# Block-masked attention into a rational feed-forward layer: the weight clamp folded into an Abs, the last tile's maxima chained in PSUM, and twelve units moved behind the switch

## The chip, the cores and the metric

The kernel runs on one core of a Trainium2 chip. Its time is the device time of one execution in microseconds; a profiled execution also gives a span, from its first to its last instruction. The engines of the core run beside each other and wait for one another through semaphores: TensorE (PE) multiplies matrices into PSUM, VectorE (DVE) and ScalarE (ACT) read and write PSUM and SBUF, GpSimd (POOL) works on SBUF alone, and SyncE (SP) issues the DMAs. PSUM has eight banks of 512 float32 columns by 128 partitions.

## What is computed

Eight batches of eight heads, 576 positions, head size 64. Attention is masked by blocks of 64 positions, and its output, 4608 tokens of 512 features, goes through a feed-forward layer of width 2048 whose activation is a rational function.

```python
scores = scale * np.matmul(q, k.transpose(0, 1, 3, 2))
mask = block_i >= block_j
scores = np.where(mask, scores, -1000000000.0)
scores = scores - np.max(scores, axis=-1, keepdims=True)
attn = np.exp(scores)
attn = attn / (np.sum(attn, axis=-1, keepdims=True) + 1e-09)
x = np.matmul(attn, v)            # then heads side by side: 4608 x 512
h = x @ w_in
P = a[0] + a[1] * h + a[2] * h**2 + a[3] * h**3
Q = 1.0 + np.abs(b[0]) * np.abs(h) + np.abs(b[1]) * h**2
out = (P / (Q + 1e-6)) @ w_out
```

The two weight matrices arrive as float64; q, k and v are float32.

## The kernel before

Every matrix product of the layer is made of three: each operand is split into a high part and the rest, and high x high, high x rest and rest x high are added in PSUM.

**The planner.** The kernel is written as operations handed to a class `Plan`: each has an engine, an estimated cost, a priority (a small number goes early) and the buffers that it reads and writes. `order()` (line 94) plays the program through with these costs: on each engine it starts the operation of the lowest number that can start, gives it its buffers, and so fixes the order of instructions on every engine. A `Buf` may take a slot of a second pool, a quota, so that one use can't take all PSUM banks: QA (5) for attention, QH (1) and QO (2) for the first product and the output of the first stage, QH1 (2), QO1 (4) and QR1 (2) for the second stage. `gate(pri, ahead)` (line 349) makes an operation wait until the attention's scores of number `pri - ahead` have been issued; the attention runs through the numbers 0 to 319, ten for each of 32 pairs of heads.

**Attention.** For a pair of heads, `load` brings q, k and v, `prep` transposes q and k on PE and splits them, and `scores` (line 443) works through five tiles of queries. A tile's scores are in one PSUM bank, those of the last tile (t = 4, 576 keys) in two pieces of 288. DVE takes the negated maximum of each piece (L467); for the last tile a third instruction (L471) takes the smaller of the two. ACT makes the Exp with this bias and the row sums (L475), POOL scales the probabilities by the reciprocal (L489, L495), PE transposes them (L516), ACT and DVE split them (L531, L533), and `pv` (line 540) multiplies them with v and writes the result to scratch in HBM (`xscr`, L572). There is one buffer of probabilities for each of the five tiles. The transposes have the number of their tile less 6 (line 501).

**Weights.** `place` (line 576) turns a block of 128 x 512 float64 weights into the two float32 parts with integer operations on the two words: ACT's Abs of the upper word (L585), a maximum with the constant WMIN on POOL (L587), then shifts and masks on DVE (L589 to L599), one more ACT and one POOL operation. There are 32 blocks: 16 for the first half of the hidden features, which stay in SBUF (`wA`), and 16 for the second half, which go to scratch.

**The layer.** The hidden features are split in halves of 8 x 128. The first stage (`ffn0`, line 665) runs beside attention: 18 chunks of 256 tokens, four units each. A unit is two groups of 12 matmuls of 256 columns into one bank (L698), the activation (`wide`, line 633: ACT L635, L636, L646, L649, L658; POOL L638, L640, L659; DVE L642 to L655), and 12 matmuls of 512 columns into the chunk's two output banks (L717). The chunk's sums go to scratch (`pscr`, L725). Units have numbers from 50 to 325 and on: the last 14 of the 72 come after the attention's end. When attention is over, `switch` (line 757) gives its SBUF to the second half's weights (`wB`, loaded at L773), two x tiles (`xx`) and one tile for stored sums (`pp`). The second stage (`ffn1`, line 780) then takes nine chunks of 512 tokens in order, each with eight units of one 128-feature group (12 matmuls of 512 columns at L805, 12 at L821); it loads the two stored sums of a chunk into the one `pp` tile (L830), adds them (L834) and stores the result (L838).

Of the kernel before, what the change touches and what calls it, by code (L numbers as in the profile page):

```python
# [23 lines left out]
CT = 256  # L24
# [11 lines left out]
WMIN = struct.unpack("<f", struct.pack("<I", (1023 - 127) << 20))[0]  # L36
# [21 lines left out]
class Op:  # L58
    __slots__ = ("eng", "c", "d", "fn", "pri", "deps", "outs", "bufs", "n", "ready", "at", "end", "seq")


LATENCY = {"PE": 90.0, "ACT": 40.0, "DVE": 40.0, "POOL": 90.0, "SP": 60.0, "-": 0.0}


class Plan:
# [5 lines left out]
    def op(self, eng, cd, fn, rd=(), wr=(), pri=0.0, after=()):  # L71
        o = Op()
        o.eng, (o.c, o.d), o.fn, o.pri, o.seq = eng, cd, fn, pri, len(self.ops)
# [14 lines left out]
        if eng in ("ACT", "DVE") and any(b.quota for b in bufs):  # L88
            o.pri -= 4
# [4 lines left out]
    def order(self):  # L94
# [16 lines left out]
        def startable(o):  # L111
            t, need = o.ready, {}
            for b in o.bufs:
                if b.slot is None:
                    need.setdefault(b.pool, []).append(0)
# [9 lines left out]
        while left:  # L125
# [41 lines left out]
            o.at = t  # L167
            if e == "SP":
# [55 lines left out]
def attn_ffn_kernel(  # L224
# [24 lines left out]
    QA, QH, QO, QH1, QO1, QR1 = (Pool([None] * n) for n in (5, 1, 2, 2, 4, 2))  # L249
# [37 lines left out]
    NM = tiles(att, 6, [128, 2, 2], F32, "nm")  # L287
# [155 lines left out]
    def scores(p, s, t):  # L443
# [5 lines left out]
        for j in range(2):  # L449
# [4 lines left out]
            bks = []  # L454
            for i, (c0, w) in enumerate(pieces(t)):
                ww = max(w, 256)
                bank = Buf(banks, QA, 1)
                bks.append(bank)

                def sc(bank=bank, c0=c0, ww=ww, kq=kq):  # L460
# [3 lines left out]
                o_ = aop("PE", mm(2, ww), sc, rd=kk, wr=[bank], pri=pri, after=kqmask[p % 2, j] if p < 2 else ())  # L464
                if not i:
                    gates[p * 10 + t * 2 + j] = o_
                aop("DVE", dve(w), lambda bank=bank, i=i, j=j, w=w: nc.vector.reduce_max(  # L467
                    out=nm.t[:nq, j, i:i + 1], in_=bank.t[:nq, :w], axis=AX.X, negate=True),
                    rd=[bank], wr=[(nm, j, i)], pri=pri)
            if t == 4:  # L470
                aop("DVE", (141, 160), lambda j=j: nc.vector.tensor_tensor(  # L471
                    out=nm.t[:, j, 0:1], in0=nm.t[:, j, 0:1], in1=nm.t[:, j, 1:2], op=ALU.min),
                    rd=[(nm, j, 1)], wr=[(nm, j, 0)], pri=pri)
            for i, (c0, w) in enumerate(pieces(t)):
                aop("ACT", act(w, True, 1, True), lambda i=i, j=j, c0=c0, w=w, bank=bks[i]: nc.scalar.activation(  # L475
                    out=pt.t[:nq, j, c0:c0 + w], in_=bank.t[:nq, :w], func=AF.Exp,
                    bias=nm.t[:nq, j, 0:1], scale=1.0, accum_out=sm.t[:nq, j, i:i + 1]),
                    rd=[bks[i], (nm, j, 0)], wr=[(pt, j, i), (sm, j, i)], pri=pri, after=first)
# [399 lines left out]
```

## Time and profile before

| | us |
|---|---|
| time, median of 3 (1412.52 to 1414.75) | 1413.2 |
| the profiled execution | 1413.04 |
| its span | 1410.8 |
| PE busy | 1270.7 (90%) |
| DVE busy | 1012.6 (72%) |
| POOL busy | 963.6 (68%) |
| ACT busy | 906.4 (64%) |

The page of the profile shows the span in forty slices of about 35 us; each digit is the busy share of an engine in tenths. Other views give busy time by stretch, by line, the waits with the instruction that ended them, and the instructions in order of time. A matmul's duration in a row includes its way through the array, and the next one starts before it ends; the work of a group of matmuls is therefore read from the length of the whole group.

### The profile page before, as it was taken

To read this page: it belongs to the slowest core of one execution; us is meant where nothing else is said; L and a number is where in the kernel's file an instruction comes from. 1 tells how busy PE (TensorE), PEld (TensorE's weight loads), DVE (VectorE), ACT (ScalarE), POOL (GpSimd) and SP (SyncE) were. 2 spreads that over 40 slices of the span, in tenths; PEclk is the share of its full clock that TensorE was granted. 3 is DMA by queue.
4 is the path that set the end of the run, shared out by engine and by line. 5 is a ranking of instruction groups with operands and counts; after the bars stand their busy time and mean duration, and the time that the engine had idled before them with its cause. 6 is when DMAs were issued, how large, how long until landed. Compare 5 with 4: busy or idle time off the path is not lost.

```text
span 1410.8 us, 23662 instructions
## 1 busy us (share of the span) xinstructions
PE 1270.7 (90%) x7616; PEld 1113.0 (79%) x7616; DVE 1012.6 (72%) x2045; ACT 906.4 (64%) x2246; POOL 963.6 (68%) x1245
## 2 busy tenths in 40 slices
PE   4767789999999999999999999678999999999996
PEld 3657688888888888888888899567888888888875
DVE  4778887777878887787886776444576667666764
ACT  4767776776777777677777677334555556555553
POOL 4789987777778778678787677334566566555653
PEclk9878999999999999999999999888999999999998
DMA  8868576666567576666765652840032323222321
GB/s 195 224 183 222 137 193 176 163 189 190 161 185 195 154 201 185 176 166 170 192 187 154 166 149 72 299 170 31 16 117 63 99 80 120 91 89 87 93 60 45
DMA packets 230811, 206.17 MB, mean 146 GB/s; under 512 B 131872, under 2 KB 189216, under 8 KB 230688
## 3 DMA queue, kind: packets, MB, share of 16 engines
q1 hardware_dynamic: 230624, 204.66, 51.5%
q8 instruction: 61, 1.00, 0.3%
q14 instruction: 62, 0.51, 0.1%
q0 software_dynamic: 64, 0.00, 0.0%
HBM read 100.67 MB, written 46.14 MB: 104 GB/s over the span
## 4 chain that ended last, share of the span: by engine, by line
PE 42%; POOL 26%; DVE 11%; ACT 8%; issue 5%; DMA 5%; SPq 1%; POOLq 0%; DVEq 0%; ACTq 0%
POOL vpl L432 3%; POOL ua L640 2%; POOL p3a L495 2%; POOL ua L587 2%; POOL gla L659 2%; PE psb L821 2%; PE psf L805 2%; PE psg L805 2%; POOL ub L587 2%; POOL glb L659 1%; PE psc L821 1%; POOL vb L638 1%; POOL ub L640 1%; POOL p2a L495 1%; PE psa L717 1%
## 5 line engine op out<-in xcount | busy, mean ns | idle before, releaser
L659 POOL TENSOR_TENSOR glb<-sa,ghb 128x512 fp32r<-128x512 f32 x62 | 80.0, 1290 | 103.5 <-ACT ghb L658 103.0
L659 POOL TENSOR_TENSOR gla<-sb,gha 128x512 fp32r<-128x512 f32 x58 | 75.0, 1292 | 66.1 <-ACT gha L658 65.7
L432 POOL TENSOR_TENSOR vpl<-vra,vph 128x256 fp32r<-128x256 f32 (+1 forms) x128 | 78.2, 619 | 22.6 <-ACT vph L430 15.9
L640 POOL TENSOR_TENSOR ub<-va,ub 128x512 f32<-128x512 f32 x63 | 82.2, 1304 | 4.8
L638 POOL TENSOR_SCALAR va<-ub,bab 128x512 f32<-128x512 f32 x63 | 49.3, 783 | 47.7 <-ACT ub L635 45.9
L640 POOL TENSOR_TENSOR ua<-vb,ua 128x512 f32<-128x512 f32 x59 | 77.4, 1313 | 4.7
L646 ACT ACTIVATE va<-ub,qcb 128x512 f32<-128x512 f32 x63 | 45.7, 725 | 53.8 <-POOL ub L640 53.7
L658 ACT CAST ghb<-sa 128x512 fp32r<-128x512 f32 x62 | 38.4, 620 | 58.6 <-DVE sa L655 58.4
L638 POOL TENSOR_SCALAR vb<-ua,bab 128x512 f32<-128x512 f32 x59 | 48.2, 818 | 39.7 <-ACT ua L635 34.7
L646 ACT ACTIVATE vb<-ua,qcb 128x512 f32<-128x512 f32 x59 | 42.7, 724 | 35.7 <-POOL ua L640 35.7
L658 ACT CAST gha<-sb 128x512 fp32r<-128x512 f32 x58 | 35.8, 617 | 39.7 <-DVE sb L655 32.3
L587 POOL TENSOR_SCALAR ua<-ua 128x512 f32<-128x512 f32 x19 | 37.7, 1987 | 9.9 <-ACT ua L585 9.5
L430 ACT CAST vph<-vra 128x256 fp32r<-128x256 f32 (+1 forms) x128 | 39.4, 324 | 4.5 <-DMA vra<-in_v_dram 3.0
L651 DVE SCALAR_TENSOR_TENSOR ub<-ub,va 128x512 f32<-128x512 f32 x27 | 20.4, 756 | 16.5 <-ACT va L649 16.4
L651 DVE SCALAR_TENSOR_TENSOR ua<-ua,vb 128x512 f32<-128x512 f32 x23 | 18.6, 810 | 12.8 <-ACT vb L649 11.0
L587 POOL TENSOR_SCALAR ub<-ub 128x512 f32<-128x512 f32 x13 | 26.2, 2018 | 0.2
L649 ACT ACTIVATE va<-va 128x512 f32<-128x512 f32 x37 | 23.5, 634 | 0.5
L642 DVE TENSOR_TENSOR sb<-sb,psh 128x512 f32<-128x512 f32 x10 | 6.8, 685 | 21.9 <-ACT sb L636 21.9
L649 ACT ACTIVATE vb<-vb 128x512 f32<-128x512 f32 x35 | 22.2, 633 | 0.6
L653 DVE SCALAR_TENSOR_TENSOR va<-ub,va 128x512 f32<-128x512 f32 x27 | 21.8, 807 | 0.4
L589 DVE TENSOR_SCALAR ua<-ua 128x512 int32<-128x512 int32 x19 | 12.8, 673 | 12.4 <-POOL ua L587 12.3
L642 DVE TENSOR_TENSOR sb<-sb,psf 128x512 f32<-128x512 f32 x10 | 6.8, 684 | 20.0 <-ACT sb L636 20.0
(1597 smaller groups left out, 5882.1 us busy)
## 6 DMA issues: line engine op xcount, KB each, us to landing
xscr<-xsa SPq DMA_DIRECT2D x32, 320.0 KB, 2.9
qra<-in_q_dram SPq DMA_DIRECT2D x64, 144.0 KB, 3.0
qra<-in_k_dram SPq DMA_DIRECT2D x64, 144.0 KB, 2.9
ppa<-pscr SPq DMA_DIRECT2D x18, 512.0 KB, 4.2
vra<-in_v_dram SPq DMA_DIRECT2D x64, 128.0 KB, 2.4
xscr<-xsa SPq DMA_DIRECT2D x32, 256.0 KB, 2.7
kqaa<-hl0a SPq DMA_DIRECT2D x48, 144.0 KB, 3.1
kqab<-hl0a SPq DMA_DIRECT2D x48, 144.0 KB, 3.1
```

What stands on the lines that cost most here:

```text
L430: aop("ACT", (0.833 * n + 110, 0.833 * n + 200), lambda vh=vh, src=src: nc.scalar.copy(out=vh, in_=src()), rd=rd, wr=[("v", i, 0)], pri=pr ...
L432: aop("POOL", pool(n, True), lambda vh=vh, vl=vl, src=src: nc.gpsimd.tensor_tensor(out=vl, in0=src(), in1=vh.bitcast(F32), op=ALU.subtract ...
L495: aop("POOL", pool(n - 64), lambda jj=jj: nc.gpsimd.tensor_scalar(out=pt.t[:nq, jj, 64:n], in0=pt.t[:nq, jj, 64:n], scalar1=rc.t[:nq, jj:j ...
L587: op("POOL", pool(512), lambda: nc.gpsimd.tensor_scalar(out=at.t, in0=at.t, scalar1=WMIN, scalar2=1.0, op0=ALU.max, op1=ALU.mult), wr=[at] ...
L638: op("POOL", pool(512, False, 2), lambda: nc.gpsimd.tensor_scalar(out=vt.t, in0=ut.t, scalar1=b1, scalar2=b0, op0=ALU.mult, op1=ALU.add), ...
L640: op("POOL", pool(512, True), lambda: nc.gpsimd.tensor_tensor(out=ut.t, in0=vt.t, in1=ut.t, op=ALU.mult), rd=[vt], wr=[ut], pri=pri)
L646: op("ACT", act(512, False, 1), lambda: nc.scalar.activation(out=vt.t, in_=ut.t, func=AF.Ln, bias=qcb), rd=[ut, "qcb"], wr=[vt], pri=pri)
L649: op("ACT", act(512, False), lambda: nc.scalar.activation(out=r0.t, in_=vt.t, func=AF.Exp, scale=-1.0), rd=[vt] if rpsum else [], wr=[r0], ...
L658: op("ACT", act(512, False), lambda: nc.scalar.copy(out=gh.t, in_=st.t), rd=[st], wr=[gh], pri=pri)
L659: op("POOL", pool(512, True), lambda: nc.gpsimd.tensor_tensor(out=gl.t, in0=st.t, in1=gh.t.bitcast(F32), op=ALU.subtract), rd=[st, gh], wr ...
L805: nc.tensor.matmul(h.t, lhsT=w[:, dc, fs], rhs=x.t[:, dc, hl, :], start=(dc == 0 and i == 0), stop=(dc == 3 and i == 2))
L821: nc.tensor.matmul(o[m].t, lhsT=g.t[:, ms], rhs=w[:, f, :], start=(f == 0 and i == 0), stop=(f == NFB - 1 and i == 2))
```

## The change

Five things change.

1. In `place` POOL's maximum (L587) goes. ACT's Abs gets a scale of 2^-112, and two masks on DVE change their constants. Costs in the planner that are marked `port=True` rise by 220 ns.
2. In `scores` the two banks of the last tile are used together: the maximum of the second is written beside the scores of the first (column 288), and one reduction over 289 columns gives the negated maximum. The minimum (L471) goes.
3. The units of chunks 15, 16 and 17 leave the first stage. `ffn1` gets a list of work: first the units of either half that the first stage left out, with the weights `wA`, then its eight own units. Its chunks run in the order 8, 0, 1, ..., 7. Chunks 15 to 17 are not stored and not added: their output is copied by ACT.
4. After the switch the first stage may use a second QH bank (`gives`).
5. Numbers change: the transposes of the probabilities move from 6 before to 3 behind their tile, operations on quota banks go 2 instead of 4 ahead, gates open 12 instead of 20 ahead, units run from 60 to 340, and the two halves of the weights from 10 to 70 (20 to 60 before) and from 90 to 270 (70 to 290).

The core of the diff:

```diff
-    def gate(pri, ahead=20):
+    def gate(pri, ahead=12):
...
-            o.pri -= 4
+            o.pri -= 2
...
+            for pl in o.gives:
+                heapq.heappush(pl.free, (t, 0))
...
-                    rd=[bank], wr=[(nm, j, i)], pri=pri)
             if t == 4:
-                aop("DVE", (141, 160), lambda j=j: nc.vector.tensor_tensor(
-                    out=nm.t[:, j, 0:1], in0=nm.t[:, j, 0:1], in1=nm.t[:, j, 1:2], op=ALU.min),
-                    rd=[(nm, j, 1)], wr=[(nm, j, 0)], pri=pri)
+                aop("DVE", dve(w), lambda b0_=bks[0], b1_=bks[1], w=w: nc.vector.reduce_max(
+                    out=b0_.t[:nq, w:w + 1], in_=b1_.t[:nq, :w], axis=AX.X),
+                    rd=[bks[1]], wr=[bks[0]], pri=pri)
+            n_ = w + (t == 4)
+            aop("DVE", dve(n_), lambda j=j, bank=bks[0], n_=n_: nc.vector.reduce_max(
+                out=nm.t[:nq, j:j + 1], in_=bank.t[:nq, :n_], axis=AX.X, negate=True),
+                rd=[bks[0]], wr=[(nm, j)], pri=pri)
...
-        pri += -6
+        pri += 3
...
-        op("ACT", act(512, False), lambda: nc.scalar.activation(out=at.t, in_=w1().bitcast(F32), func=AF.Abs),
-           rd=[st], wr=[at], pri=pri)
-        op("POOL", pool(512), lambda: nc.gpsimd.tensor_scalar(
-            out=at.t, in0=at.t, scalar1=WMIN, scalar2=1.0, op0=ALU.max, op1=ALU.mult), wr=[at], pri=pri)
+        op("ACT", act(512, False), lambda: nc.scalar.activation(
+            out=at.t, in_=w1().bitcast(F32), func=AF.Abs, scale=2.0 ** -112), rd=[st], wr=[at], pri=pri)
...
-    split_weights(wA, 0, NFA, [20 + 40.0 * i / NPLA for i in range(NPLA)], False)
-    split_weights(wscr, NFA, NFB, [70 + 220 * i / NPLB for i in range(NPLB)], True)
-    E0, E1, HOLD = 50, 325, 14
+    split_weights(wA, 0, NFA, [10 + 60 * i / NPLA for i in range(NPLA)], False)
+    split_weights(wscr, NFA, NFB, [90 + 180 * i / NPLB for i in range(NPLB)], True)
+    E0, E1 = 60, 340
+    EARLY = ()
+    U0 = [list(range(EARLY[c] if c < len(EARLY) else 4 if c < NCH - 3 else 0)) for c in range(NCH)]
...
-    sw = op("-", (0, 0), switch, after=att_ops, pri=0)
+    sw = op("-", (0, 0), switch, after=att_ops, pri=0, gives=[QH, QR])
...
+        work = [(hf, u) for u in range(NFA // 2) for hf in range(2) if u not in U0[2 * c + hf]]
+        work += [(2, f) for f in range(NFB)]
...
+                else:
+                    op("ACT", act(512), lambda m=m, ob=ob, osb=osb: nc.scalar.copy(
+                        out=osb.t[:, m * 512:(m + 1) * 512], in_=ob.t), rd=[ob], wr=[(osb, m)], pri=pe)
...
-    for c in range(NCH1):
-        ffn1(c, 400.0 + c * NFB, 1.0)
+    base = 400.0
+    for c in (NCH1 - 1, *range(NCH1 - 1)):
+        base = ffn1(c, base, 1.0)
```

The loads of the first chunk's x in the second stage have the number 320, ahead of the weight loads from 330 on; those of later chunks are four numbers ahead of their work.

More of the change, by code (lines that the diff above doesn't have):

```diff
@@ L114, in startable @@
                 if b.slot is None:
-                    need.setdefault(b.pool, []).append(0)
+                    need.setdefault(b.pool, []).append(0 if b.quota else b.keep)
                     if b.quota:
@@ L685, in ffn0 @@
             x.parts = parts
-        gs_ = []
-        for u in range(NFA // 2):
-            pri = pris[u]
+        gs_ = {}
+        for u, pri in zip(units, pris):
             h = Buf(banks, QH)
@@ L816, in ffn1 @@
+        last = {m: max(n for n, (hf, _) in enumerate(work) if hf in (2, m // 2)) for m in range(4)}
+        for n, (hf, f) in enumerate(work):
+            gh, gl = gs_[n]
             for m in range(4):
-                def second(f=f, gh=gh, gl=gl, m=m):
-                    woh, wol = late["w"][2:]
-                    ms = slice(m * 128, (m + 1) * 128)
-                    for i, (g, w) in enumerate(((gl, woh), (gh, woh), (gh, wol))):
-                        nc.tensor.matmul(o[m].t, lhsT=g.t[:, ms], rhs=w[:, f, :],
-                                         start=(f == 0 and i == 0), stop=(f == NFB - 1 and i == 2))
@@ L824, in ffn1, with second @@
-                op("PE", mm(3, 512), second, rd=[gh, gl] + [("wB", i, f - f % 2) for i in (2, 3)],
-                   wr=[o[m], "oseq"], pri=base + (f + 0.5) * step)
-        pe = base + NFB * step
+                if hf not in (2, m // 2):
+                    continue
+                def second(f=f, hf=hf, gh=gh, gl=gl, m=m, a=m not in seen, z=n == last[m]):
+                    woh, wol = late["w"][2:] if hf == 2 else wA[2:]
+                    for j in range(1 if hf == 2 else 2):
+                        c0, ff = (m * 128, f) if hf == 2 else (j * CT + m % 2 * 128, 2 * f + j)
+                        for i, (g, w) in enumerate(((gl, woh), (gh, woh), (gh, wol))):
+                            nc.tensor.matmul(o[m].t, lhsT=g.t[:, c0:c0 + 128], rhs=w[:, ff, :],
+                                             start=(a and i == 0 and j == 0), stop=(z and i == 2))
@@ L827, in ffn1 @@
+                seen.add(m)
+                op("PE", mm(3 if hf == 2 else 6, 512), second, rd=[gh, gl] + (
+                    [("wB", i, f - f % 2) for i in (2, 3)] if hf == 2 else wkeys(0, 2 * f, "o") + wkeys(0, 2 * f + 1, "o")),
+                    wr=[o[m], "oseq"], pri=base + (n + 0.5) * step)
+        pe = base + len(work) * step
         for hf in range(2):
-            part, osb = Buf(PT1), Buf(OS)
             cc = 2 * c + hf
-            op("SP", sp(512, dims=2), lambda cc=cc, part=part: nc.sync.dma_start(
-                out=part.t.rearrange("p (m d) -> p m d", m=2), in_=pscr[cc]),
-                rd=[("pscr", cc)], wr=[part], after=[sw], pri=pe - 4 * step)
@@ L833, in ffn1 @@
[L833 to L837 removed]
+            osb = Buf(OS)
+            if U0[cc]:
+                part = Buf(PT1)
+                op("SP", sp(512, dims=2), lambda cc=cc, part=part: nc.sync.dma_start(
+                    out=part.t.rearrange("p (m d) -> p m d", m=2), in_=pscr[cc]),
+                    rd=[("pscr", cc)], wr=[part], after=[sw], pri=pe - 4 * step)
```

126 lines of the change are left out of this document (67 added, 59 removed).

## The prediction

> **What bounds the kernel now.** I read the forty slices of the page first, then the busy time by stage, then what TensorE (PE) waits for, then the timelines of the two places where it stands still.
>
> ```profile
> span 1410.8 us, 23662 instructions
> PE   4767789999999999999999999678999999999996
> POOL 4789987777778778678787677334566566555653
> PEclk9878999999999999999999999888999999999998
> ...
> 0.00:100.00 100.00, 62.45 (x354) 52.58 (x354) 65.60 (x173) 59.86 (x188) 67.81 (x108) 0.88 0.81 204
> 100.00:200.00 100.00, 79.30 (x492) 70.48 (x493) 88.47 (x186) 69.95 (x194) 90.25 (x110) 0.86 0.67 179
> ...
> 200.00:884.50 684.50, 642.51 (x4558) 587.60 (x4557) 537.98 (x1224) 506.66 (x1434) 518.90 (x773) 1.00 0.62 170
> 884.50:996.10 111.60, 84.74 (x465) 73.57 (x464) 46.51 (x63) 41.74 (x67) 41.29 (x36) 0.86 0.45 158
> 996.10:1401.40 405.30, 401.69 (x1753) 328.80 (x1751) 272.80 (x401) 228.20 (x368) 245.35 (x220) 1.00 0.26 80
> ```
>
> The columns of the second part are the stretch and its length, then busy time and instructions of PE, PE's weight loads, VectorE (DVE), ScalarE (ACT) and GpSimd (POOL), then granted clock, DMA share and GB/s. The reader is to see five stages. From 200 us to the end of attention (884.5) PE is 94% busy at full clock: 42 us are idle. From 996.1 it is 99% busy. So PE bounds both, and work on other engines counts there only where PE waits for it. Between them lies a hole, and in the first 200 us PE stands idle for 58 us while POOL and DVE are the fullest engines. Every gain must come from the first 200 us, the hole, the 42 us, or the end.
>
> **The hole.** What it costs is its length less the work done in it. The price of work is a first-stage matmul group (24 of 256 columns) and a group of 12 of 512 columns:
>
> ```profile
> 903.07 2.88 PE psh L698 x24
> ...
> 998.87 2.72 PE psd L805 x12
> ...
> 884.50:996.10 111.60, 39.59 (x312) 39.11 (x312) 0.86 0.45 158
> ...
> 884.50:996.10 111.60, 47.44 (x152) 34.48 (x150) 0.86 0.45 158
> ...
> PE psb L717 <- POOL gla L659: 10.0, 2, 5.7
> PE psd L717 <- POOL gla L659: 6.2, 2, 5.7
> PE psf L717 <- POOL glb L659: 5.7, 1, 5.7
> PE psa L717 <- POOL gla L659: 3.2, 1, 3.2
> PE psb L698 <- DMA xa<-xscr: 1.7, 1, 1.7
> ...
> 895.00:900.00 5.00, 2.32 (x6) 0.60 1.09 356
> 915.00:920.00 5.00, 4.06 (x10) 0.51 1.05 412
> 985.00:990.00 5.00, 5.00 (x22) 0.68 0.00 0
> ```
>
> The third and fourth rows are line 698 and line 717 alone in the hole: 312/24 = 13 units' first products, 13 x 2.88 = 37.4 us, and 152/12 = 12.7 units' second products, 12.7 x 2.72 = 34.5 us. That is 71.9 us of work in 111.6 us: 39.7 us lost. The waits name 26.8 us of it: PE waits for the last GpSimd step of a unit (L659), because only one unit's first product can be open at a time (QH holds one bank) and its chain over ACT, POOL and DVE is longer than the matmuls beside it. The other 12.9 us are clock: after each of the five long gaps PE runs at about half speed for some microseconds (0.60, 0.51, 0.68), 12.9/5 = 2.6 us each. The Trainium skill, "TensorE: Matmul & The Clock Gate", Part 1, says that the clock is halved after an idle window of about 3.4 us and comes back after as long a busy one; the trace agrees after the 5.7 us gaps, and shows the drop after the 3.2 us gap as well. I price every such gap from the rows.
>
> **Part 1: twelve units moved behind the switch.** The units of chunks 15 to 17 are no longer run in the first stage, and PE's work stays the same: 12 x (2.88 + 2.72) = 67.2 us leave the hole and open the second stage, where two units are open at once and r0 has banks of its own. That stage loses little now: 72 units x 5.44 = 391.7, plus two late groups of L717 (5.4), are 397.1 us of work in 405.3 us, so 2.1% is lost, and 67.2 us more cost 1.4 us more. ACT, DVE and POOL cover is there: DVE, the fullest, has 272.8/72 = 3.8 us for a unit of 5.44.
>
> What is late next is the first load. The second stage now opens with chunks 16 and 17, whose tokens are of the last batch, so its x tile can't come before the switch.
>
> ```profile
> 884.55 0.36 SPq L572 DMA_DIRECT2D xscr<-xsa  x1
> 887.10 0.60 SPq L773 DMA_DIRECT2D wihb<-wscrih  x1
> ...
> 916.33 8.70 SPq L790 DMA_DIRECT2D xxb<-xscr  x8
> ...
> xxa<-xscr SPq DMA_DIRECT2D x8, 512.0 KB, 7.7
> ```
>
> The first load behind the switch was issued 2.55 us after the last attention output; an issue of x takes 8.70/8 = 1.09 us, and one of 512 KB lands in 7.7 us. Four of them: 2.55 + 3 x 1.09 + 7.7 = 13.5 us until the first new unit can begin. They are issued ahead of the 16 weight loads, which now wait behind them on SP's queue; those are needed only after eight opening units, 8 x 5.6 = 45 us, and 16 x 0.52 MB at the 356 GB/s of the row of 895 us take 24 us. PE's cover for the 13.5 us are first-stage units left over. Unit n now has the number 60 + 4.67n and attention ends at 319, so by number units 56 to 59 are left, 4 x 5.6 = 22 us of work, though with stalls of the kind above; the second QH bank that the switch gives helps. If the gates let them all run early, almost nothing is left. I take one gap of 5.7 us with its clock, 8.3 us lost; the ends are 3 (the longest single wait for gl without clock loss) and 18.7 (the whole 13.5 uncovered, with two clock losses). Gain 39.7 - 8.3 = 31.4, from 21 to 37. By the skill's window the clock would cost 3.4/2 = 1.7 us (an estimate from that page) rather than 2.6, so 32.3 in place of 31.4.
>
> **Part 2: the end.** The second stage now ends with chunks 14 and 15, and 15 has no stored part to add.
>
> ```profile
> 1401.02 0.39 PE L821 MATMUL psa<-wolb,ghb 128*128 128x512 f32 x1
> ...
> 1400.78 0.33 SPq L830 DMA_DIRECT2D ppa<-pscr  x1
> 1404.96 0.69 DVE L834 TENSOR_TENSOR osb<-psg,ppa 128x512 f32<-128x512 f32 x1 [4.21 <-DMA ppa<-pscr]
> 1406.27 0.38 SPq L838 DMA_DIRECT2D out_dram<-osb  x1
> ```
>
> Now PE is done at 1401.4, but the part of the last half is loaded into the one buffer (ppa) only at 1400.78, and the adds wait 4.21 us for it. Afterwards a ScalarE copy follows the last matmul; priced like such an add (0.69), it lets the store leave near 1402.2 instead of 1406.27. What is late next is the store itself. Gain 4.0, from 0 to 4.2.
>
> **Part 3: the clamp.** One POOL instruction (L587) of each of 32 weight blocks goes. Its work is done by a scale in the Abs that ScalarE runs anyway; the masks on DVE change their constants alone.
>
> ```profile
> 0.00:100.00 100.00, 15.61 (x8) 0.88 0.81 204
> 100.00:200.00 100.00, 17.46 (x9) 0.86 0.67 179
> ...
> sum 884.50, POOL 63.93; mean POOL 7.10
> ...
> DVE ub L589 <- POOL ub L587: 7.4, 5, 3.0
> DVE ua L589 <- POOL ua L587: 6.0, 5, 2.2
> ...
> PE psa L516 <- POOL p3a L495: 3.7, 6, 1.7
> ```
>
> The first three rows are L587 alone: 33.1 us of the first 200 us and 63.9 in all, 2.0 us each. In the first 200 us POOL falls from 158 to 125 busy us. DVE was held 13.4 us there by the clamp, but it has 154 us of its own in this stretch and loses nearly none: at its present 88% that alone is 154/0.88 = 175 us, a gain of at most 25. The upper end is 33 (all of POOL's time), the lower 0 (DVE, ACT's start and the DMAs at a share of 0.81 keep the pace; the first units also start at number 60 instead of 50, leaving PE less to fill with). I take 12, the near half of DVE's bound.
>
> From 200 to 884.5 us POOL loses 30.9 us of 518.9. PE's waits there are for many steps of POOL's queue, the row of p3a being the longest group of the softmax, and less load shortens them; PE's 42 idle us are the ceiling.
>
> **Part 4: the chained maximum, and the order.** Of three DVE instructions per head of the last tile, the small minimum goes; the second reduction takes one column more and now waits for the first, which stands before it on the same engine.
>
> ```profile
> sum 884.50, DVE 24.71; mean DVE 2.75
> ```
>
> This is L471 alone: 64 times, 0.39 us. Ends for the chain: all 24.7 us of DVE saved, or none, where the new wait costs what the minimum did. Queued behind a waiting reduction are DVE's next steps, with ACT's Exp behind them; DVE is 79% busy in this stage, so neither end lies on PE's path for long. The planner's numbers change too: transposes come 9 later, quota steps 2 later, gates open at 12 ahead instead of 20. The trace before shows none of these orders; half of the 42 idle us either way (20) is my bound, and 0 the value, as the work is the same. For 200 to 884.5 us together I take a gain of 6, about a seventh of the idle time for POOL's 6% less load with the shorter DVE chain; ends -14 and 25.
>
> **Sum.** 31.4 - 1.4 + 4.0 + 12 + 6 = 52.0. The span 1410.8 becomes 1358.8. The profiled execution took 1413.04, 2.2 more than its span and within 0.2 of the median 1413.2, so the time is 1361.0.
>
> **The rivals.**
> - *Only the switch and the end pay.* DVE and the DMAs hold the first 200 us, and PE's other waits close over the freed POOL time. For it: DVE at 88%, DMA at 0.81. Against it: 13.4 us in which DVE itself waited for the clamp. 31.4 - 1.4 + 4.0 = 34.0: 1379.
> - *The gap is moved, not closed.* The x load is uncovered (18.7 lost) and the attention stage gives nothing: 21 - 1.4 + 4.0 = 23.6, so 1389.6. For it: nothing loads x earlier. Against it: units left over by number.
> - *The start opens up.* POOL was the real limit: 25 at the start and 20 in the middle, with the rest 79: 1334.
> - *Slower: late transposes hold the probabilities.* Each of the five probability tiles has one buffer; the next pair's Exp into it waits until this pair's transposes have read it. They move 9 numbers back, of 10 that a pair spans, and 6 are left before the next pair's scores of that tile. If that delays each of 32 pairs by d, the loss is 32d; it eats the whole gain from d = 52/32 = 1.6 us. At 2.5 us it is 80, and the time 1441. For it: PE's waits at L516 are already the commonest of the middle. Against it: six numbers are more than half a pair of slack, and PE always has units to run.
>
> **How the numbers follow.** The forecast (1345 to 1372) gets 0.52, the switch alone 0.2, the moved gap 0.08, the open start 0.12, late transposes 0.08, of which 0.06 above the time before. The range 1335 to 1392 takes in the first three and part of the fourth. A measurement of this kernel tells about 0.2% (2.8 us) from no change; only a mixture of late transposes and the gains falls within that, 0.03. Faster 0.91, slower 0.06.
>
> **What would show it.** In the new profile: no stretch between the end of attention and the end of the second stage with PE under 90% beyond one gap of about 6 us, ended by a DMA into xx or by gl; PE at 99% for about 460 us; the last store within 1.5 us of the last matmul; POOL's total near 900 us; PE idle for some 46 us rather than 58 in the first stretch up to the same pair. I am wrong if PE's idle time in the middle grows past 42 us (order), if the first 200 us stay as they are (DVE), or if the gap at the switch is above 10 us.

## The result, and the profile after

The changed kernel takes 1333.3 us, the median of four runs (1322.7 to 1334.3), beside 1413.5 us of the kernel before on the same chip: a ratio of 0.942 with a 95% interval of 0.937 to 0.946 (ratios are of means, so the one run of 1322.7 puts it a little under 1333.3/1413.5). The forecast was 1361.0 in a range from 1335 to 1392. The direction is right; the gain is 80 us where 52 were forecast, and the time lies below the range by 1.7 us.

First the page after: the span, the totals, three of the engines in slices of 33 us and the granted clock.

```profile
span 1330.8 us, 23509 instructions
PE 1244.9 (94%) x7616; PEld 1101.8 (83%) x7616; DVE 991.5 (74%) x1975; ACT 905.4 (68%) x2246; POOL 898.6 (68%) x1213
PE   4867789999999999999999999999999999999997
POOL 4556678768787777777776777555656666666554
PEclk9878899999999999999999999999999999999999
```

From the seventh slice to the last but one PE's row is all nines: the 6, 7 and 8 that marked the hole are gone, and so are the 8s in the clock row there. POOL's first slices, 4789987 before, are 4556678. Its total of 898.6 us is what the prediction expected (near 900).

The busy times by stage, after: the first two rows are split where the sixth pair's output has been stored (175.81 us) and where attention ends (846.67); the last runs from there to the last matmul.

```profile
0.00:175.81 175.81, 124.72 (x754) 109.82 (x755) 125.01 (x311) 116.87 (x348) 100.23 (x179) 0.86 0.77 200
175.81:846.67 670.86, 644.43 (x4624) 593.80 (x4623) 541.22 (x1202) 515.63 (x1460) 509.46 (x776) 1.00 0.65 177
...
846.70:1325.80 479.10, 475.35 (x2242) 398.18 (x2240) 325.25 (x463) 271.94 (x439) 288.89 (x260) 1.00 0.29 93
```

And before, split at the same two events (188.48 and 884.55):

```profile
0.00:188.48 188.48, 132.03 (x790) 114.31 (x791) 144.94 (x338) 123.42 (x361) 147.60 (x203) 0.87 0.75 195
188.48:884.55 696.07, 652.28 (x4614) 596.40 (x4613) 547.14 (x1244) 513.10 (x1452) 529.36 (x787) 0.99 0.62 169
```

The sixth pair is done 12.7 us earlier, but less of the layer runs ahead of it (754 matmuls in all instead of 790), so this is not all gain; the account of the prediction takes it apart. In the middle PE stands idle for 26.4 us (670.86 - 644.43) instead of 43.8. Behind attention it is 99.2% busy (475.35 of 479.10).

The timeline after, at the switch and at the end (start, duration, engine, line, instruction; in brackets the idle time ahead of it and what ended it):

```profile
846.67 0.36 SPq L574 DMA_DIRECT2D xscr<-xsa  x1
849.34 2.58 SPq L791 DMA_DIRECT2D xxa<-xscr  x4
858.13 0.50 PE L813 MATMUL psc<-xxa,wiha 128*128 128x256 f32 x2 [0.68 <-DMA xxa<-xscr]
...
1325.79 0.39 PE L835 MATMUL psc<-wolb,ghb 128*128 128x512 f32 x1
1326.21 0.58 ACT L859 COPY osa<-psc 128x512 f32<-128x512 f32 x1
1326.83 0.37 SPq L861 DMA_DIRECT2D out_dram<-osa  x1
```

The x tile is there 11.5 us after the last attention output (858.13 - 846.67), and PE waits 0.68 us for it: first-stage work that was left over filled the rest of the time. The last store leaves 0.65 us after the last matmul. PE's waits behind attention, all of them, after:

```profile
PE psd L835 <- POOL glb L662: 1.5, 1, 1.5
PE psd L835 <- POOL gla L662: 1.4, 1, 1.4
PE psc L813 <- DMA xxa<-xscr: 0.7, 1, 0.7
```

The clock around the wait for x, after, in five microseconds of the busy times:

```profile
855.00:860.00 5.00, 4.32 (x30) 3.82 (x29) 2.90 (x6) 1.97 (x3) 3.03 (x3) 1.00 1.05 367
```

It stays at 1.00. The waits are 3.6 us, where the prediction's fence of the hole alone has 26.8.

**Two numbers for each run.** Units of the layer can run before or after the end of attention, so the end alone says little. *Attention* below is its end less 2.88 us for each first and 2.72 us for each second product done by then: what attention costs with its own work. *Behind* is the span less the end and less the work left (5.44 us for each of 72 second-stage groups, and 2.88 and 2.72 for what is left of the rest): what is lost there. After, 1.3 firsts and 4 seconds are left over beside the twelve moved units and the 72 groups: 391.7 + 67.2 + 14.7 = 473.6 us in 1330.8 - 846.67 = 484.1, so 10.5 are lost.

| kernel | time, us | ratio to before (95%) | attention | behind |
|---|---|---|---|---|
| before | 1413.5 | | 558.2 | 57.7 |
| after | 1333.3 | 0.942 (0.937 to 0.946) | 525.4 | 10.5 |
| forecast | 1361.0 | | 540.2 | 23.7 |

The forecast's row is its own terms: 18 (12 + 6) off attention, 34 (31.4 - 1.4 + 4.0) off what is behind. It missed by 14.8 in the one and 13.2 in the other: 28.0, the whole miss in the span (1358.8 against 1330.8).

### The profile page after: what moved, and what is told of

Same layout as the page of the kernel before. It is cut to its first block, busy times and chain, and to the rows that moved or that the text cites. A ratio compares the mean times of both kernels' runs of the same rounds, so it can differ in the third digit from the quotient of the medians.

```text
span 1330.8 us, 23509 instructions
## 1 busy us (share of the span) xinstructions
PE 1244.9 (94%) x7616; PEld 1101.8 (83%) x7616; DVE 991.5 (74%) x1975; ACT 905.4 (68%) x2246; POOL 898.6 (68%) x1213
## 4 chain that ended last, share of the span: by engine, by line
PE 62%; POOL 10%; ACT 8%; DMA 7%; DVE 7%; issue 3%; SPq 2%; POOLq 0%; ACTq 0%; DVEq 0%
PE psc L835 3%; PE psg L810 3%; PE psb L810 3%; PE psh L835 3%; PE psd L835 3%; PE psa L835 2%; PE psd L700 2%; PE pse L835 2%; PE psf L835 2%; PE psf L719 2%; PE pse L810 2%; PE psf L810 2%; PE psa L810 2%; POOL p4a L497 1%; PE psc L700 1%
## 5 line engine op out<-in xcount | busy, mean ns | idle before, releaser
L434 POOL TENSOR_TENSOR vpl<-vra,vph 128x256 fp32r<-128x256 f32 (+1 forms) x128 | 79.4, 627 | 26.5 <-ACT vph L432 17.4
L662 POOL TENSOR_TENSOR glb<-sa,ghb 128x512 fp32r<-128x512 f32 x61 | 79.2, 1298 | 16.0 <-ACT ghb L661 15.8
L662 POOL TENSOR_TENSOR gla<-sb,gha 128x512 fp32r<-128x512 f32 x63 | 81.6, 1294 | 12.4 <-ACT gha L661 11.9
L642 POOL TENSOR_TENSOR ua<-vb,ua 128x512 f32<-128x512 f32 x65 | 84.5, 1300 | 5.0
L648 ACT ACTIVATE vb<-ua,qcb 128x512 f32<-128x512 f32 x65 | 47.3, 728 | 48.2 <-POOL ua L642 48.1
L661 ACT CAST ghb<-sa 128x512 fp32r<-128x512 f32 x61 | 37.9, 621 | 17.6 <-DVE sa L658 17.6
L654 DVE SCALAR_TENSOR_TENSOR ua<-ua,psb 128x512 f32<-128x512 f32 x19 | 13.1, 688 | 25.1 <-ACT psb L652 25.1
L654 DVE SCALAR_TENSOR_TENSOR ua<-ua,psg 128x512 f32<-128x512 f32 x18 | 12.4, 688 | 25.6 <-ACT psg L652 25.6
L637 ACT ACTIVATE ub<-psb 128x512 f32<-128x512 f32 x23 | 13.8, 601 | 25.0 <-PE psb L810 21.1
L637 ACT ACTIVATE ub<-psg 128x512 f32<-128x512 f32 x21 | 12.6, 598 | 22.2 <-PE psg L810 18.3
L810 PE MATMUL psg<-xxa,wihb 128*128 128x512 f32 x80 | 24.6, 389 | 0.0
L644 DVE TENSOR_TENSOR sb<-sb,psb 128x512 f32<-128x512 f32 x24 | 16.4, 685 | 7.8 <-ACT sb L638 7.8
L810 PE MATMUL psb<-xxa,wihb 128*128 128x512 f32 x72 | 22.2, 389 | 0.0
```

What stands on the lines that cost most here:

```text
L434: aop("POOL", pool(n, True), lambda vh=vh, vl=vl, src=src: nc.gpsimd.tensor_tensor(out=vl, in0=src(), in1=vh.bitcast(F32), op=ALU.subtract ...
L642: op("POOL", pool(512, True), lambda: nc.gpsimd.tensor_tensor(out=ut.t, in0=vt.t, in1=ut.t, op=ALU.mult), rd=[vt], wr=[ut], pri=pri)
L648: op("ACT", act(512, False, 1), lambda: nc.scalar.activation(out=vt.t, in_=ut.t, func=AF.Ln, bias=qcb), rd=[ut, "qcb"], wr=[vt], pri=pri)
L654: op("DVE", dve(512), lambda: nc.vector.scalar_tensor_tensor(out=ut.t, in0=ut.t, scalar=QC, in1=r0.t, op0=ALU.add, op1=ALU.mult), rd=[r0], ...
L661: op("ACT", act(512, False), lambda: nc.scalar.copy(out=gh.t, in_=st.t), rd=[st], wr=[gh], pri=pri)
L662: op("POOL", pool(512, True), lambda: nc.gpsimd.tensor_tensor(out=gl.t, in0=st.t, in1=gh.t.bitcast(F32), op=ALU.subtract), rd=[st, gh], wr ...
```

## The experiments

Eighteen kernels, each beside the kernel before. The theories, as the expectations name them: A, the clamp cost so much because it loads GpSimd; B, the new numbers of the order did it; C, the chain on VectorE to the Exp held attention; D, the clamp was planned at the wrong length (667 ns; about 1930 measured); E, the minimum waits for GpSimd's way into SBUF; F, it costs as a third instruction; S, this order is a lucky one. In before, after, e1, e2 and e3 the planner hands out an operation's buffers in an arbitrary order of addresses; in all others in the order in which they were made, so that their order of work can differ a little more than the edit says. No run has the changed kernel unmoved in that second order. Comparisons of e4, e4b, e10, e11 and e12 with it therefore hold this difference too, and so does the step from e5 to e3; those within the moved positions 61 and 62 do not.

### One part taken back

`e1_clamp_back` puts the clamp back, planned as before; `e2_min_back` the minimum; `e3_numbers_back` the numbers of point 5 of the change (those of the weights too, the 220 ns of point 1, and a buffer that the change keeps free for the weights' words); `e4_units_back2` the twelve units, at the same pace. A first build of the latter, in the arbitrary order of addresses, gave no time.

```diff
e1
-            out=at.t, in_=w1().bitcast(F32), func=AF.Abs, scale=2.0 ** -112), rd=[st], wr=[at], pri=pri)
+            out=at.t, in_=w1().bitcast(F32), func=AF.Abs), rd=[st], wr=[at], pri=pri)
+        op("POOL", pool(512), lambda: nc.gpsimd.tensor_scalar(
+            out=at.t, in0=at.t, scalar1=WMIN, scalar2=1.0, op0=ALU.max, op1=ALU.mult), wr=[at], pri=pri)
...
e2
...
+                aop("DVE", (141, 160), lambda j=j: nc.vector.tensor_tensor(
+                    out=nm.t[:, j, 0:1], in0=nm.t[:, j, 0:1], in1=nm.t[:, j, 1:2], op=ALU.min),
+                    rd=[(nm, j, 1)], wr=[(nm, j, 0)], pri=pri)
...
e3
-PORT = 220.0
+PORT = 0.0
...
-            o.pri -= 2
+            o.pri -= 4
...
-    def gate(pri, ahead=12):
+    def gate(pri, ahead=20):
...
-        pri += 3
+        pri += -6
...
-    E0, E1 = 60, 340
+    E0, E1 = 50, 325
...
e4
-    U0 = [list(range(EARLY[c] if c < len(EARLY) else 4 if c < NCH - 3 else 0)) for c in range(NCH)]
+    U0 = [list(range(EARLY[c] if c < len(EARLY) else 4)) for c in range(NCH)]
...
-    for c in (NCH1 - 1, *range(NCH1 - 1)):
+    for c in range(NCH1):
```

> The changed kernel with the maximum on GpSimd put back (and the Abs without its scale, the two old masks); everything else as changed. Attention ended 37.9 us earlier after the change (846.7 instead of 884.6), 33 us of it less time lost by TensorE. Theory A, the clamp did most of it by freeing GpSimd: attention ends at 865 to 875, the time is near 1355, and the first six pairs take some 12 us longer again (188 instead of 176 us). Theory B, the new numbers of the order did it: attention ends within 8 us of 846.7, the time is at most 1342.

> The changed kernel with two separate maxima and the small minimum for the last tile put back. VectorE gets some 20 us of busy time back and loses the wait of the second reduction for the first. Theory A and B alike: VectorE is not on TensorE's path, 1333 to 1340. A third theory C, that VectorE's chain to the Exp holds the attention: attention ends 10 us or more later, 1345 or more.

> The changed kernel with the old numbers of the order: transposes 6 ahead of their tile, quota operations 4 ahead, gates 20 ahead, units from 50 at the old pace, weights from 20 to 60 and 70 to 290, no added planner cost for shared ports, and a weight block no longer keeping an output buffer free. Clamp, chained maximum and moved units stay. Theory A: attention ends within 8 us of 846.7, the time is at most 1342. Theory B: attention ends at 865 to 880, the time is 1350 to 1365.

> The changed kernel with all 72 units in the first stage again, at the same pace (so the last 12 come behind attention), and the second stage in the order 0 to 8; the second QH bank after the switch stays. (Here and in what follows the buffers of an operation get their slots in the order in which they were made.) By the two traces the time lost behind attention fell from 57.3 to 10.2 us. If the move of the units did it: 1375 to 1382, with the waits for gl back at the first stage's second products. If the second QH bank alone closes the gaps: at most 1350.

| kernel | time, us | ratio to before (95%) | attention | behind |
|---|---|---|---|---|
| e1_clamp_back | 1385.9 | 0.980 (0.977 to 0.983) | 577.1 | 11.0 |
| e2_min_back | 1351.8 | 0.955 (0.954 to 0.957) | 544.9 | 11.1 |
| e3_numbers_back | 1352.5 | 0.956 (0.954 to 0.957) | 529.9 | 25.9 |
| e4_units_back2 | 1360.5 | 0.963 (0.960 to 0.966) | 520.0 | 43.3 |

The columns part cleanly: clamp and minimum cost time in attention and none behind it; units cost it behind attention, and numbers mostly there. The clamp alone costs 52.6 us, nearly three times what start and middle were forecast to gain together, and far more than A had expected (1355). The minimum came out as C has it. The numbers came out at B's time but not in B's place: attention ends at 856.5 us where B named 865 to 880. The units came out between the two values named for them. PE's longest waits behind attention with the units back show the old gap:

```profile
PE psc L704 <- DMA xa<-xscr: 9.1, 1, 9.1
PE psd L839 <- POOL gla L666: 4.1, 1, 4.1
PE psb L723 <- POOL gla L666: 3.0, 1, 3.0
```

And the stretch around it, in the same kernel:

```profile
846.00:870.00 24.00, 13.12 (x60) 10.17 (x58) 5.64 (x8) 6.30 (x10) 6.19 (x5) 0.81 1.06 392
...
861.00 2.93 SPq L687 DMA_DIRECT2D xa<-xscr  x4
```

Attention ends at 841.30 us in this kernel. The first of the three chunks that are left needs x of the last pair; the second half of it (`xa`) is issued only at 861.00, behind twelve of the weight loads on SP's queue. It comes 9.1 us late, and PE works 13.1 of 24 us at a clock of 0.81. In the changed kernel the first x behind the switch is issued at 849.34, ahead of the weight loads, and left-over units cover it.

### From before to after, in steps

`e5_switch_alone` is the changed kernel with clamp, minimum and numbers of before: the moved units and the second QH bank alone. `e4b_units_and_bank_back` is e4 without the bank, and with the second stage of before.

```diff
e4b
-    sw = op("-", (0, 0), switch, after=att_ops, pri=0, gives=[QH, QR])
+    sw = op("-", (0, 0), switch, after=att_ops, pri=0)
```

> The kernel before the change with the moved units and the second QH bank alone: clamp, minimum and all numbers of the order as before. If the parts add up, it keeps what was won behind attention by the two traces, 47 us, and nothing before it: attention ends at 880 to 890, the time is 1363 to 1371. If the move needs the other parts (leftover units, a different pace): 1378 or more, as by the prediction's first two terms.

> The changed kernel with all 72 units in the first stage and without the second QH bank after the switch; the second stage as before the change. With the bank kept the same step had cost 27 us (1360.5). If the bank gives the other 20 of the 47 us: 1376 to 1384. If the bank gives nothing: 1358 to 1364.

| step | time, us | ratio to before (95%) | attention | behind |
|---|---|---|---|---|
| before | 1413.5 | | 558.2 | 57.7 |
| + units and bank (e5) | 1379.6 | 0.976 (0.973 to 0.978) | 558.1 | 22.3 |
| + clamp and minimum gone (e3) | 1352.5 | 0.956 (0.954 to 0.957) | 529.9 | 25.9 |
| + numbers (after) | 1333.3 | 0.942 (0.937 to 0.946) | 525.4 | 10.5 |
| e4b_units_and_bank_back | 1372.2 | 0.970 (0.967 to 0.973) | 522.2 | 52.4 |

The first step gains 33.9 us (35.7 against the runs of before beside it); the forecast for switch and end was 34.0, and the rival in which only these pay said 1379. The second gains 27.1 where 18 were forecast, all of it in attention (28.2). The third gains 19.2 where 0 was the value, 15.4 of it behind attention. Of the units' gain, e4 and e4b put about 9 us on the bank together with the new program of the second stage (52.4 - 43.3; e4b takes back both, so they aren't told apart) and 33 on the units (43.3 - 10.5). e4b, too, came out between the values named for it.

What the numbers mend behind attention is seen in PE's waits there with the old ones (e3):

```profile
PE psb L835 <- POOL glb L662: 4.5, 1, 4.5
PE psc L813 <- DMA xxa<-xscr: 1.9, 3, 0.7
PE pse L835 <- POOL gla L662: 1.9, 1, 1.9
PE psh L835 <- POOL glb L662: 1.2, 1, 1.2
```

Most of them are for units' last GpSimd steps that come late. All waits together are 11.1 us, 7.5 more than after. The other 8 of the 15.4 us are longer busy time of PE for the same work, at a granted clock of 0.99 behind attention instead of 1.00. Part of that begins at the switch, where x comes in three pieces; the rows are the four microseconds with the three waits, and two microseconds just behind:

```profile
863.60:867.60 4.00, 2.08 (x11) 1.25 (x9) 2.16 (x4) 1.47 (x3) 0.12 (x1) 0.98 1.05 402
868.00:870.00 2.00, 2.00 (x11) 2.00 (x11) 0.00 (x0) 0.10 (x1) 1.28 (x1) 0.50 1.11 405
```

No wait there is longer than 0.7 us, and the clock still falls to 0.50. The prediction had looked for the effect of the numbers in attention only. Which of the numbers does it isn't shown; they were taken back together.

### The clamp: work or plan

`e10_clamp_true_cost` is e1 with the clamp planned at 2000 ns; `e7_before_true_cost` does that to the kernel before; `e11_cheap_step` puts a shorter instruction in the clamp's place, a multiplication by one, planned as before.

```diff
e10, e7
-        op("POOL", pool(512), lambda: nc.gpsimd.tensor_scalar(
+        op("POOL", (2000.0, 2030.0), lambda: nc.gpsimd.tensor_scalar(
e11
+            out=at.t, in0=at.t, scalar1=1.0, scalar2=1.0, op0=ALU.mult, op1=ALU.mult), wr=[at], pri=pri)
```

> The kernel with the clamp put back (1385.9, 53 us slower than the changed one), with one number more changed: the planner is told 2000 ns for the clamp, near its measured 1930, where it had been told 667. Theory D, the price is that of an order planned with a wrong duration: most of the 53 us come back, 1335 to 1352. Theory A, the price is GpSimd's 64 us of work and the longer chain of a block, whatever the planner knows: 1370 or more.

> The changed kernel with another GpSimd step where the clamp was, a product with 1.0 twice (it changes no value), whose form took 0.78 to 0.82 us elsewhere and which the planner holds for 0.67. 32 x 0.8 = 26 us of GpSimd work and the same step in the chain of a block, but nearly rightly planned. Theory A, price in proportion to the work: 53 x 26/64 = 21, so 1350 to 1360. Theory D: at most 1342.

> The kernel before the change with one number changed: the planner is told 2000 ns for the clamp instead of 667. No instruction is added or removed. Theory D, much of what the removal of the clamp gained was the end of a wrongly planned order: attention ends 20 us or more earlier than 884.6 and the time is 1375 to 1395. Theory A, GpSimd's work counted: within 6 us of 1413.

| kernel | time, us | ratio to before (95%) | attention |
|---|---|---|---|
| e1_clamp_back | 1385.9 | 0.980 (0.977 to 0.983) | 577.1 |
| e10_clamp_true_cost | 1349.1 | 0.955 (0.953 to 0.957) | 542.1 |
| e11_cheap_step | 1354.4 | 0.958 (0.956 to 0.960) | 549.5 |
| e7_before_true_cost | 1402.7 | 0.992 (0.990 to 0.993) | 551.8 |

The clamp itself in e1 (shortest, median and longest, in ns):

```profile
L591 POOL TENSOR_SCALAR ua<-ua x17: 1922/1931/2426, 28.3 to 676.9; 128x512 f32<-128x512 f32 x17
L591 POOL TENSOR_SCALAR ub<-ub x15: 1922/1932/2487, 44.2 to 706.7; 128x512 f32<-128x512 f32 x15
```

VectorE's waits for it in e1:

```profile
DVE ua L593 <- POOL ua L591: 23.3, 16, 2.5
...
DVE ub L593 <- POOL ub L591: 13.5, 11, 2.3
```

VectorE's waits for it in e10 (the same instructions, told their length):

```profile
DVE ua L597 <- POOL ua L595: 4.3, 7, 1.8
DVE ub L597 <- POOL ub L595: 4.1, 4, 1.8
```

With 667 ns planned, the planner puts the shift that needs the clamp's result too early into VectorE's fixed order, and VectorE stands for 36.8 us with all that is behind it; told the length, it stands for 8.4 us, and GpSimd's busy time up to the end of attention is the same (674.9 and 674.6 us). So of the 52.6 us that the put-back costs, e10 leaves 15.8, which A alone can't explain. In the old order the same correction gained 10.8 us (12.7 against the runs beside it), and the wait, of both buffers together, fell from 23.3 to 9.3; that is more than A named and less than D did. D alone doesn't hold either: the shorter step of e11 (0.74 us on average, 667 ns planned) still cost 21.1 us, where D expected nearly nothing and A, by its share of the work, 21. How much of the clamp's price in the old order was load, how much plan, isn't settled: the next section shows that single orders differ by as much.

### How much is this one order

`c59`, `e8_control` and `c62` are the changed kernel with the units' numbers moved by -1, +1 and +2.

```diff
-    E0, E1 = 60, 340
+    E0, E1 = 59, 339      (c59; 61, 341 in e8; 62, 342 in c62)
```

> The changed kernel with the units' numbers moved by one (61 to 341 instead of 60 to 340): the same instructions, planned anew. It tells how much a new plan alone moves the time, beside which the price of each part is to be read. If plans are alike: 1328 to 1338. If one new plan can cost what the cheap step did (21 us): 1345 or more.

> The changed kernel with the units' numbers moved by minus one (59 to 339). So far: 1333.3 unmoved, 1354.0 moved by one, 1332.7 by two. If the usual plan is near 1333 and the move by one the odd one out: 1328 to 1340. If plans scatter evenly: 1345 or more as likely as not.

> The changed kernel with the units' numbers moved by two (62 to 342). Theory S, the change's own plan is a lucky one of many that scatter by some 20 us: 1345 to 1362, like the move by one (1354). Rival, the move by one was an unlucky plan: 1328 to 1340.

| kernel | time, us | ratio to before (95%) | attention | behind |
|---|---|---|---|---|
| c59 | 1349.9 | 0.955 (0.951 to 0.960) | 535.3 | 16.6 |
| after (60) | 1333.3 | 0.942 (0.937 to 0.946) | 525.4 | 10.5 |
| e8_control (61) | 1354.0 | 0.956 (0.954 to 0.959) | 543.9 | 13.6 |
| c62 | 1332.7 | 0.944 (0.940 to 0.948) | 526.8 | 11.7 |

The same instructions at numbers one apart differ by up to 21 us, as much as a part of the change; e8 and c59 came out as the expectation of scatter has it, c62 as its rival. The mean of the four is 1342.5, and the changed kernel lies 9 us below it. Against this scatter the numbers' effect in attention (529.9 in e3, 525.4 to 543.9 here) can't be told; behind attention it can: 25.9 and 22.3 with the old ones, 10.5 to 16.6 with the new ones. The ten other kernels with the new numbers and the moved units, the parts of attention put back or not, lie between 10.3 and 15.2 behind it.

So clamp and minimum were put back at other positions too: `k61`, `k62` are e1 moved by 1 and 2, `m61`, `m62` are e2 moved.

> The changed kernel moved by one (1354.0) with the clamp put back and planned at 667 ns. If the clamp's 53 us are its own: 1390 to 1410. If some 20 of them were the first plan's luck: 1378 to 1390.

> The changed kernel moved by two (1332.7) with the clamp put back and planned at 667 ns. It cost 53 us unmoved and 41 us moved by one. If that is its price: 1372 to 1388. If the unmoved plan was unusual: 1365 or less.

> The changed kernel moved by one (1354.0) with the two maxima and the minimum of SBUF operands put back. If the minimum costs what it did in the first plan (18 us, more than scatter): 1366 to 1378. If those 18 us were scatter: 1342 to 1362, on either side of 1354.

> The changed kernel moved by two (1332.7) with the two maxima and the minimum of SBUF operands put back. It cost 18.5 us unmoved and 8 us moved by one. If it has a price of its own: 1340 to 1353. If it was scatter: 1332 or less.

| position | as it is | clamp back | minimum back |
|---|---|---|---|
| 60 | 1333.3 | 1385.9 (+52.6) | 1351.8 (+18.5) |
| 61 | 1354.0 | 1395.3 (+41.3) | 1362.1 (+8.1) |
| 62 | 1332.7 | 1376.1 (+43.4) | 1338.7 (+6.0) |

The ratios to before are 0.989 (0.983 to 0.994) and 0.974 (0.970 to 0.978) for k61 and k62, 0.965 (0.956 to 0.974) and 0.947 (0.941 to 0.953) for m61 and m62. The clamp, planned too short, costs 41 us or more at each position and 46 on average; VectorE waits for it for 33.0 us in k61 and 32.0 in k62, beside 36.8 in e1. That is the price of its own that the expectations of k61 and k62 name. The minimum costs 11 on average; m61 and m62 came out at or below the lower end of a price of its own. The kernel is slower with it at all three positions, but at 61 and 62 the intervals overlap those of e8 and c62, so only its price at 60 is clear of the noise of the runs.

### The minimum: a third instruction, or its operands

`e12_min_psum` has the minimum as e2 has it, three instructions per head, but leaves the second maximum in PSUM, so that one of its two operands comes from there. `p61` is e12 moved by 1.

```diff
...
+                    out=bank.t[:nq, w:w + 1] if i else nm.t[:nq, j, i:i + 1], in_=bank.t[:nq, :w], axis=AX.X, negate=True),
...
+                    out=nm.t[:, j, 0:1], in0=b1_.t[:nq, w:w + 1], in1=nm.t[:, j, 0:1], op=ALU.min),
```

> The kernel with two maxima and a minimum (1351.8), where now the second maximum is left in PSUM, so that the minimum has one operand in PSUM and one in SBUF. The minimum with both operands in SBUF took 0.13 us at best and 1.3 at worst before the change, and 1.3 us is the length of a GpSimd product. Theory E, it waits for GpSimd to leave a way into SBUF that two SBUF operands need: without that its longest is under 0.3 us and the time falls to 1333 to 1342. Theory F, the third instruction itself or its place in the chain costs: the time stays at 1347 to 1355.

> The changed kernel moved by one, with the minimum that has one operand in PSUM. By theory E (the wait for the way into SBUF) it is faster than the minimum with two SBUF operands in the same move, by 8 us or more; in any case its longest minimum is under 0.3 us. If the 18 us were scatter: within 8 us of it, or slower.

| position | after's two reductions | minimum, both in SBUF | minimum, one in PSUM |
|---|---|---|---|
| 60 | 1333.3 | 1351.8 (0.955, 0.954 to 0.957) | 1334.2 (0.944, 0.942 to 0.947) |
| 61 | 1354.0 | 1362.1 (0.965, 0.956 to 0.974) | 1344.2 (0.952, 0.947 to 0.958) |

Moving one operand gains 17.6 and 17.9 us (at 61 the two intervals overlap a little, but each run of the one is faster than each of the other), as E expected; the third instruction as such costs nothing that these runs can tell. The minimum's durations (shortest, median, longest, ns) in e2:

```profile
L472 DVE TENSOR_TENSOR nmf<-nmf x10: 147/533/1269, 148.4 to 800.1; 128x1 f32<-128x1 f32 x10
```

The same with one operand in PSUM (e12):

```profile
L476 DVE TENSOR_TENSOR nmd<-psf,nmd x5: 145/151/158, 48.4 to 825.4; 128x1 f32<-128x1 f32 x5
```

And in the timeline of the kernel before, what the long ones stand beside:

```profile
632.12 1.29 POOL L659 TENSOR_TENSOR glb<-sa,ghb 128x512 fp32r<-128x512 f32 x1
632.16 1.26 DVE L471 TENSOR_TENSOR nma<-nma 128x1 f32<-128x1 f32 x1
633.46 0.50 ACT L475 ACTIVATE p4a<-psf,nma 128x288 f32<-128x288 f32 x1 [1.03 <-DVE nma L471]
...
683.03 1.30 DVE L471 TENSOR_TENSOR nmd<-nmd 128x1 f32<-128x1 f32 x1
683.03 1.28 POOL L659 TENSOR_TENSOR glb<-sb,ghb 128x512 fp32r<-128x512 f32 x1
```

And the same line over the whole of before, for one of its buffers:

```profile
L471 DVE TENSOR_TENSOR nmb<-nmb x10: 130/155/1270, 97.8 to 767.8; 128x1 f32<-128x1 f32 x10
```

An instruction of one element per partition runs until GpSimd's subtraction of 512 beside it is over, and the Exp waits for it. This is no matter of two examples: of the 30 minima of more than 0.3 us in before, 26 end within 0.03 us of the end of a GpSimd instruction, and in e2 all 27 do. In e12, 41 of the 64 minima run wholly inside a GpSimd instruction, and none takes more than 0.16 us. VectorE's time for all 64 falls from 23.6 us in e2 to 9.6. The Trainium skill, "GPSIMD Engine Reference", section 1 (Specifications), says that GpSimd's way into SBUF is shared with VectorE and contended by VectorE instructions with two SBUF inputs; the trace agrees, and shows that the small size of the VectorE instruction gives no protection: 0.14 us become 1.26.

## Why the prediction was right, and where it was wrong

**The switch's sum was right, by terms that offset each other.** "Gain 39.7 - 8.3 = 31.4" and the end's 4.0, with 1.4 off, made 34.0; e5, which has just this part, gains 33.9. That is partly luck. "I take one gap of 5.7 us with its clock, 8.3 us lost" was too dark: in e5 PE waits 1.9 us around the switch, at a granted clock of 1.00. The second stage was priced too low: PE waits there 7.6 us for late GpSimd steps, and the clock is 0.93 in the last 55 us of e5. Gap and stage together lose 17.2 us in e5 (22.3 less the 5.1 behind the last matmul), where 8.3 + 8.2 + 1.4 = 17.9 were forecast. In the finished kernel the gap is 0.68 us. An issue of x takes 2.58/4 = 0.64 us instead of 1.09, and the tile comes after 11.5 us instead of 13.5. The cover is 14.7 us of left-over work, less than the 22 counted by number, but none of the stalls set against it came. The stage's 1.4 us more weren't paid either: gap and stage together lose 5.9 us, where the stage alone lost 8.2 before. The end gained 4.8 (from 9.4 us between last matmul and end of span to 4.6) for 4.0.

**Where it failed first: "half of the 42 idle us either way (20) is my bound, and 0 the value, as the work is the same."** The numbers gave 19.2 us, at the bound's edge, and at another place than the one it was drawn from. The 42 us are PE's idle time in attention; what the numbers mended, 15.4 us, is behind attention, where the prediction let only the switch and the end act. Part of the 19.2 is the one order that was hit: on the mean of four positions, behind is 13.1, so some 11 of it stands.

**Where it failed second: "For 200 to 884.5 us together I take a gain of 6, about a seventh of the idle time for POOL's 6% less load".** The middle gave 25.1 us, at the upper end of the term's -14 to 25. At the sixth pair's end before had done 18.8 us of the layer's products and after 13.9, since its units start later. Less this work the start went from 169.7 to 162.0 us, a gain of 7.7 where 12 were forecast; PE's idle time there fell by 5.4 us (56.5 to 51.1), where 12 were named. The other 25.1 of the 32.8 us came behind the sixth pair: PE's idle time fell by 17.4 there, and the rest is shorter busy time for the same work, at a granted clock of 1.00 instead of 0.99. The steps tell the parts: from e5 to e3, which takes out clamp and minimum at the old numbers, the start gains 12.4 us, as forecast, and the middle 15.8 (single orders, these too); the new numbers then take 4.8 back at the start and give 9.3 in the middle, which is within the scatter of single orders.

So the term failed for clamp and minimum already. For the clamp it went by GpSimd's load alone. In the new order the larger part of the price is another, 36.8 of 52.6 us: an instruction nearly three times as long as planned, ahead of waiting instructions in an order that is fixed. In the old order, the one that was forecast, correcting the length gained 10.8 to 12.7 us. That is enough for what the term missed there, but the minimum's price below is too, and no run parts the two in the old order. The prediction had VectorE's wait for the clamp in the first 200 us (13.4 us); over the whole of attention it is 23.3 us, and the 9.9 beyond 200 us are missing from the middle's term. The kernel's own estimate and the trace had both lengths, 667 and about 2000 ns; the prediction didn't put them beside each other.

**"Neither end lies on PE's path for long"**, of the minimum, failed too: put back, it costs 6 to 18.5 us, of which 18.5 is clear of noise. The row of 0.39 us on average hid durations from 0.13 to 1.30, and the long ones have an Exp behind them.

**What the forecast could not have known.** The scatter between neighbouring orders. In spans, attention lies 7.5 us and behind 2.6 below the mean of the four positions: 10 of the 28 us by which the forecast missed. That the time fell just below the range is therefore luck: the mean of the four positions, 1342.5, lies inside it, though with the same terms wrong. A range for a kernel whose order comes from such a planner needs some 10 us on either side for that alone. The rival "the start opens up" gave 1334, and was left at the range's edge with a chance of 0.12; its time was right and its reasons half so: the 20 in the middle came (25.1), the 25 at the start didn't (7.7), and 13 more behind attention stand in their place.

**The rivals that fell.** Late transposes: a loss of 1.6 us or more for each pair can't be there where attention ends 38 us earlier and PE stands idle less; their number wasn't changed by itself. The moved gap: 0.68 us. The rival in which only the switch pays named the time of e5, but the rest of the change adds 46 us to it.

## What to carry to other kernels

Where an order of instructions is fixed from estimated lengths, compare each estimate with the trace before pricing an edit: an operation planned too short costs the wait of everything behind it, and correcting its length was worth 37 us in one order here and 11 in another. When two orders are compared at an event, take off the other work that each has done by then. Look for the effect of a reordering at the ends of stages as well as inside them, and measure a part at two or three neighbouring orders, since a single one can flatter it by as much as it is worth. Open a stage with work whose operands are already there, and keep one operand of a small VectorE instruction in PSUM where GpSimd works on long rows beside it.

## What the runs showed of the hardware

- A VectorE minimum of 128x1 with both operands in SBUF took up to 1.30 us beside a GpSimd subtraction of 128x512, as long as the subtraction itself; with one operand in PSUM it took 0.14 to 0.16 us. Of the 30 minima of at most 0.2 us in before, 9 ran wholly inside a GpSimd tensor_scalar and none inside a GpSimd tensor_tensor.
- Three waits of 0.62 to 0.66 us within 4 us, in which PE was busy for 2.08 us, were followed by a granted clock of 0.50 (e3, at 868 us); a single wait of 0.68 us left it at 1.00 (after, at 858 us).
- GpSimd's tensor_scalar on 128x512 float32 took 1.93 us with a maximum and a multiplication, but 0.62 us with two multiplications, median each (the first in e1's row above). The e11 row:

```profile
L593 POOL TENSOR_SCALAR ua<-ua x17: 611/623/1122, 29.8 to 653.6; 128x512 f32<-128x512 f32 x17
```
